# Sink attention and a multiplicative FFN on one core: the sink values by eight small transfers and a head mask, and a new order of pieces, loads and tasks

## The chip, the cores and the metric

The kernel runs on one core of one Trainium2 chip. The metric is the device time of one execution in microseconds. Three timed runs of the kernel before are given, and one profiled execution, from which all views below are taken.

## The reference

Four batches of eight heads, 768 positions, 64 numbers to a head. Each query sees the first four keys (the sinks) and the 128 keys up to itself. The result of all heads, 3072 rows of 512, goes through a multiplicative feed-forward layer whose last two matrices are not separated by a nonlinearity.

```python
scores = scale * np.matmul(q, k.transpose(0, 1, 3, 2))
keep = (pos[None, :] < n_sink) | ((rel >= 0) & (rel < window))   # n_sink = 4, window = 128
a = softmax(np.where(keep, scores, -1e9))
x = np.matmul(a, v)                    # then rows of 512: all heads of one position
h = (x @ w1) * (x @ w2) @ w3           # 512 -> 1024 -> 1024
out = h @ w_out                        # 1024 -> 512, all in float32
```

## The kernel before, in words

**Stages.** The kernel multiplies w3 and w_out once into one matrix, `w3o` (1024 x 512). For that each of the eight row blocks of w3 is transposed on the PE (`fold_w3`, L408), copied to SBUF by the DVE as `w3t` (L413; two of them lie in free room of the tiles `kN` and `qN` of batch 1), and multiplied with the rows of w_out (`fold_mm`, L438, into PSUM tiles `ph` and `pw`). Then, for each batch: the keys and queries are transposed (batches 0 and 1 on the PE, L211, with a copy L213; batches 2 and 3 by transposing DMAs, L218), the scores are computed (`sc`, L261 and L282), the ScalarE (ACT) takes the exponential (L266, L286), the DVE applies the window mask (L270, L290), the values are multiplied in (`av`, L314 and L351), the DVE divides by the sum, and the result is transposed to `xT` (by the PE for batch 0 and a transposing DMA, L378, for the others). Two "gates" a block, `pg` (L391), give x@w1 and x@w2; ACT copies the one and the DVE multiplies it with the other (L395, L398). At last `project` multiplies with `w3o` (`po`, L452), and the output goes out by a DMA from SyncE (SP, L459).

**Sinks.** Scores against the four sink keys of all heads come from `sink_scores` (L243). The sink values of batch b lie in `vs`, one row of 128 for each of the sinks of each head: head pair r and its half e have rows 32r+4e to 32r+4e+3, zero elsewhere, with a column for the sum. They are made in `sink_values`: one PE matmul `vp` (L232) with a 0/1 matrix `pick` spreads the first four rows of `vN` to all groups of rows, and the DVE multiplies with the head mask `ones_s` (L234).

**Loads.** SP first issues nine transfers of 512 KB, the `raws`: four pieces of w_out (two row blocks each) and five row blocks of w3, in float32, to tiles that are not used yet (`homes`: `ab`, `kN`, `qN`, `kqT`). ACT or DVE casts each to bfloat16 (L418). All other loads are issued by GpSimd (POOL) with a cast on the way, in the order of the list `order`: the blocks of 128 positions of q, k and v, the other three blocks of w3, w1 and w2. POOL begins once the fifth of the raws has landed (`hold`, L201).

**The order of the work.** Each step is a `task` with its engine times, its predecessors and a priority. `plan` goes through the tasks and lets each engine take the one that can start first by the planner's own cost numbers; `landings` says when the planner thinks that loads arrive, and `keep_busy` (L466) puts matmuls on zeros, `pz`, into gaps at the start. `PACE` holds score tasks apart. What `plan` gives is written out as a fixed order of instructions for PE, ACT, DVE and SP, and each engine works through its own list in that order. So an engine that waits with one instruction holds up all that stand behind it.

Of the kernel before, what the change touches and what calls it, by code (L numbers as in the profile page):

```python
# [21 lines left out]
def kernel(  # L22
# [13 lines left out]
    nc = tc.nc  # L36
# [16 lines left out]
    CHUNKS = [[(256 * i, 256 * i + 256) for i in range(3)]] * 2 + [[(0, 384), (384, 768)]] * (B - 2)  # L53
    XPOSE = (2, 3)
    BLOCKS = ((0, 0), (0, 1))
# [71 lines left out]
    def load(what, *i):  # L127
# [21 lines left out]

    nudge = {}  # L150

# [21 lines left out]
    nc.vector.memset(maskt[:], 1.0)  # L173
    nc.vector.memset(pick[:], 0.0)
    for b in range(B - 1):
# [53 lines left out]
    def sink_values(b):  # L229

        vp = ps_mm.tile([P, H, D], FP32, tag="mm", name="vp")
        nc.tensor.matmul(vp[:], pick[:], vN[b][:, 0, :, 0:D], start=True, stop=True)  # L232
        yield
        nc.vector.tensor_mul(vs[b][:, :, 0:D], vp[:],  # L234
                             ones_s[:].rearrange("p (h o) -> p h o", o=1).to_broadcast([P, H, D]))
        yield
# [187 lines left out]
    def folded(i):  # L424
        return ("fm", i, len(FM[i]) - 1)
# [42 lines left out]

    arrive = {}

    def service(what, *i):
# [8 lines left out]

    def landings(taken, RAW=2.0, POOL=3.0, DGE=1.3, RAMP=(0.6, 0.95, 0.85, 0.9)):

        queues = {"sp": [(RAW, 1.28, 1.0, [("raw",) + x[:3]]) for x in raws],
                  "pool": [(gen, us, 1.8, keys) for x in order for gen, us, keys in service(*x)]}
# [4 lines left out]
        while any(at[n] < len(q) for n, q in queues.items()):  # L489
# [17 lines left out]
            for n in busy:  # L507
                i = int(now - RAW) if now >= RAW else 0
                share = 1.0 if len(busy) == 1 else 0.5 if small not in "kqv" else 0.79 if n == "sp" else 0.13
                left[n][at[n]] -= 0.02 * share * (RAMP[i] if i < len(RAMP) else 1.0)  # L510
                if left[n][at[n]] <= 0.0:
                    lag, keys = queues[n][at[n]][2:]
                    for key in keys:
                        arrive[key] = now + lag
                    if n == "pool":
                        landed.append(now + lag)
                    at[n] += 1
# [11 lines left out]
    made = {}  # L529
    for n, ((what, i0, i1, e), ap) in enumerate(zip(raws, casts)):  # L530
        task(("c", what, i0), n, cast(e == "act", *ap), [(e, 1.04 if e == "act" else 0.69)],
             loads=[("raw", what, i0, i1)])
        made.update({(what, i): ("c", what, i0) for i in range(i0, i1)})

    def need(what, i):
        return ([made[what, i]], []) if (what, i) in made else ([], [(what, i)])

    for i in range(KFF):
        for h in range(2):
            j0, j1 = 4 * h, 4 * h + 4  # L540
            needs = [need("w3", i)]
# [20 lines left out]
    for b in range(B):  # L562
        for t in range(NT):
# [3 lines left out]
            for kb in kbs:  # L567
                if b in XPOSE:
                    for n, src, dst in (("k", kN[b], kT[b]), ("q", qN[b], qT[b])):
# [7 lines left out]
            if t == 0:  # L577
                task(("sk", b), 0, sink_keys(b), [("dve", 0.2)], [("sc", b, 1, 0)])
                task(("sv", b), 2, sink_values(b), [("pe", 0.22), ("dve", 0.7)],
                     [("av", b - 2, NP - 1, NT - 1), ("av", b, 1, 0)] if b >= 2 else [], [("v", b, 0)], "mm")  # L580
            else:
# [3 lines left out]
                elif t == 1:  # L585
                    more = [(n, b, kb) for n in (("tdk", "tdq") if b in XPOSE else ("tpk",)) for kb in (4, 5)]
                    task(("ss", b, 1), -1, sink_scores(b, 1, NT), [("pe", 0.225), ("act", 0.6)],
                         qk + more + [("sk", b)], ring="mm", started=[("sc", b, 1, 1)])
# [21 lines left out]
            for r in range(NP):  # L610
                after = list(qk)
                if b >= 2 and t == 0:
                    after.append(("g", b - 2, len(CHUNKS[b - 2]) - 1, KFF - 1, 1))
                lead = r % 2 == 0
# [20 lines left out]
    for b in range(B):  # L635
        for c, (t0, t1) in enumerate(CHUNKS[b]):
            last_t = (t1 - 1) // 256
            us = 0.65 * (t1 - t0) / 384
            for dt in range(KFF):
                n = dt * P // 256  # L640
                pr = 1000 + 200 * b + 10 * c + dt
                war = [("p", b - 2, NB - 1)] if b >= 2 else []
                task(("g", b, c, dt, 0), pr + 0.5, gate(b, c, dt, 0), [("pe", us), ("act", 0.2 + us / 2)],
                     ([("xd", b, last_t, 0), ("xd", b, last_t, 1)] if (b, last_t) in X_XPOSE else
                      [("xt", b, NP - 2, last_t)]) + war, [("w1", n), ("w2", n)], "mm",
                     [("g",) + gates[-2] + (1,)] if len(gates) > 1 else [])
# [3 lines left out]
            for m in range(t0 // P, t1 // P):  # L650
                cuts = (0, DM // 2, 3 * DM // 4, DM) if (b, m) == (B - 1, NB - 1) else (0, DM)
                for n0, n1 in zip(cuts, cuts[1:]):
# [3 lines left out]
                          ("act", 0.1) if n0 > DM // 2 else ("sp", SP_US)],  # L656
                         [("g", b, c, KFF - 1, 1), *[folded(i) for i in range(KFF)]], ring="mm")

# [10 lines left out]
    def plan(emit):  # L669
# [16 lines left out]
        def pe_pick():  # L686
            best = None
            for k in tasks.values():
# [16 lines left out]
                if k["paced"]:  # L705
                    busy = max(0.0, free["act"] - free["pe"]) + sum(q[2] for q in queue["act"])
                    est = max(est, free["pe"] + busy - BACKLOG, last_sc + (PACE[k["name"][1]]))
                wait = est - free["pe"]
# [124 lines left out]
```

## Time and profile before

| | us |
|---|---|
| timed runs: median (lowest, highest) | 198.28 (197.68, 198.59) |
| profiled execution: time | 197.16 |
| profiled execution: span from first to last instruction | 195.5 |
| PE busy | 187.9 (96%) |
| DVE, ACT, POOL busy | 115.2, 104.2, 75.5 |
| granted TensorE clock | 1.0 throughout |

The profiled execution takes 1.7 us more than its span, and it is 1.1 us below the median of the timed runs. A row of the timeline gives start, length, engine, line, operation and what it reads and writes; a length of several matmuls is that of the group, and the last of a group overlaps the next, so that what PE spends is read from one start to the next. In brackets stands how long the engine was idle before, and who released it. PEld is the loading of weights, which runs ahead of PE. The chain of waits lists pieces that led to the end, in order of time.

### The profile page before, as it was taken

Reading aid. Unit: us, or ns where it says so; the run is one execution under the profiler, and the core shown is the slowest. Engines: PE = TensorE matmul, PEld = TensorE weight load, DVE = VectorE, ACT = ScalarE, POOL = GpSimd, SP = SyncE. Lnnn points to the kernel's source line nnn. Section 1 sums busy time; section 2 is a strip of 40 time slices with the busy share of each in tenths; the row PEclk is TensorE's granted clock in tenths of the full one; section 3 lists DMA queues with packets and bytes.
Section 4 is the critical chain, followed back from the end, with each engine's and each line's share of the span. In section 5 each row is a group of like instructions: output and inputs, shape, how many; then the busy total and the mean of one; then the engine's idle time right before and its main releaser. Section 6 shows DMA issues by size and latency. Waiting matters only on the chain.

```text
span 195.5 us, 4615 instructions
## 1 busy us (share of the span) xinstructions
PE 187.9 (96%) x1818; PEld 123.4 (63%) x1831; DVE 115.2 (59%) x276; ACT 104.2 (53%) x176; POOL 75.5 (39%) x104
## 2 busy tenths in 40 slices
PE   7689999999999999999999999999999999999993
PEld 2245566888776687888886555566666666644443
DVE  4456696755989888678575426678788344410000
ACT  4242569635776876565565646657583333333232
POOL 5189967689999953433553330000000000000000
PEclk9999999999999999999999999999999999999999
DMA  6999999999999999999999999999220200014334
GB/s 225 401 362 156 179 162 197 194 159 154 155 150 183 180 176 114 156 159 145 137 155 155 149 159 191 239 208 155 49 54 2 57 0 0 0 57 161 143 134 152
DMA packets 107429, 29.14 MB, mean 149 GB/s; under 512 B 98448, under 2 KB 102928, under 8 KB 107408
## 3 DMA queue, kind: packets, MB, share of 16 engines
q0 software_dynamic: 79520, 12.33, 90.3%
q1 hardware_dynamic: 27744, 16.46, 40.6%
q8 instruction: 14, 0.23, 0.5%
q10 hardware_dynamic: 144, 0.07, 0.1%
q14 instruction: 7, 0.06, 0.1%
HBM read 29.36 MB, written 6.29 MB: 182 GB/s over the span
## 4 chain that ended last, share of the span: by engine, by line
PE 86%; DMA 7%; POOL 3%; DVE 1%; issue 1%; SPq 1%; ACT 0%; DVEq 0%
PE pg L391 39%; PE po L452 21%; PE av L351 6%; PE sc L261 5%; DMA ab<-in_moe_w_dram 4%; PE pw L438 4%; DMA qN<-in_q_dram 3%; PE ph L438 3%; PE tp L211 2%; PE tp L408 2%; PE av L314 1%; PE sc L282 1%; POOL vN L108 1%; POOL qN L108 1%; POOL kN L108 1%; PE sp L243 1%
## 5 line engine op out<-in xcount | busy, mean ns | idle before, releaser
L391 PE MATMUL pg<-xT,w_sb 128*128 128x256 bf16 (+1 forms) x640 | 91.5, 294 | 0.0
L391 PEld LDWEIGHTS <-w_sb 128*128 128x128 bf16 x640 | 59.7, 98 | 20.2 <-issue 0.9
L398 ACT COPY a_sb<-pg 128x256 f32<-128x256 f32 (+1 forms) x80 | 33.2, 415 | 40.2 <-PE pg L391 22.7
L395 DVE TENSOR_TENSOR ab<-a_sb,pg 128x256 bf16<-128x256 f32 (+1 forms) x80 | 37.8, 472 | 25.5 <-PE pg L391 21.2
L452 PE MATMUL po<-w3o,ab 128*128 128x512 bf16 (+2 forms) x200 | 42.7, 362 | 0.4
L266 ACT ACTIVATE ex<-sc 128x1024 bf16<-128x1024 f32 (+1 forms) x40 | 38.0, 962 | 5.7 <-PE sc L261 3.9
L452 PEld LDWEIGHTS <-ab 128*128 128x128 bf16 x208 | 19.1, 98 | 20.6 <-issue 0.6
L270 DVE TENSOR_TENSOR am<-ex,maskt 128x1024 bf16<-128x1024 bf16 (+1 forms) x40 | 25.4, 646 | 5.3 <-ACT ex L266 5.2
L108 POOL DMA_DIRECT2D kN<-in_k_dram x24 | 22.4, 931 | 12.8 <-DMA qN<-in_q_dram 10.1
L456 ACT COPY w_sb<-po 128x512 f32<-128x512 f32 (+2 forms) x25 | 14.1, 564 | 24.2 <-PE po L452 24.2
L108 POOL DMA_DIRECT2D qN<-in_q_dram x24 | 22.1, 921 | 9.9 <-DMA vN<-in_v_dram 7.4
L108 POOL DMA_DIRECT2D vN<-in_v_dram x24 | 21.9, 912 | 7.2 <-DMA kN<-in_k_dram 5.1
L358 DVE TENSOR_TENSOR xn<-av,rec 128x256 bf16<-128x256 f32 x40 | 17.0, 425 | 1.4
L351 PE MATMUL av<-vN,am 128*128 128x65 bf16 x296 | 16.7, 193 | 0.0
L351 PEld LDWEIGHTS <-am 128*128 128x128 bf16 x296 | 14.4, 97 | 2.1 <-DVE am L270 0.2
L355 DVE RECIPROCAL rec<-av 128x4 f32<-128x4 f32 x40 | 7.2, 179 | 10.3 <-PE av L351 9.9
L456 DVE COPY w_sb<-po 128x128 f32<-128x128 f32 x1 | 0.3, 292 | 19.7 <-ACT w_sb L456 19.7
L261 PE MATMUL sc<-kqT 64*128 64x128 bf16 (+1 forms) x216 | 11.6, 238 | 0.0
L351 PE MATMUL av<-vs,es 128*128 128x130 bf16 x56 | 11.1, 220 | 0.0
L213 DVE COPY kqT<-tp 128x1024 bf16<-128x1024 bf16 x12 | 8.3, 689 | 3.2 <-PE tp L211 3.1
L438 PE MATMUL ph<-wo_sb,w3t 128*128 128x512 bf16 x31 | 8.0, 380 | 2.0 <-ACT wo_sb L418 1.3
L286 ACT ACTIVATE ex<-sc 128x1024 bf16<-128x1024 f32 x7 | 7.0, 1026 | 5.3 <-PE sc L282 5.3
(71 smaller groups left out, 136.0 us busy)
## 6 DMA issues: line engine op xcount, KB each, us to landing
out_dram<-w_sb SPq DMA_DIRECT2D x23, 256.0 KB, 5.0
kN<-in_k_dram POOLq DMA_DIRECT2D x24, 128.0 KB, 8.0
qN<-in_q_dram POOLq DMA_DIRECT2D x24, 128.0 KB, 8.1
vN<-in_v_dram POOLq DMA_DIRECT2D x24, 128.0 KB, 7.9
w_sb<-in_moe_w_dram POOLq DMA_DIRECT2D x9, 256.0 KB, 8.6
ab<-in_moe_w_out_dram SPq DMA_DIRECT2D x3, 512.0 KB, 6.2
ab<-in_moe_w_dram SPq DMA_DIRECT2D x3, 512.0 KB, 7.0
kN<-in_moe_w_out_dram SPq DMA_DIRECT2D x1, 512.0 KB, 9.3
```

Of the source, the lines that this page charges most:

```text
L108: nc.gpsimd.dma_start(out=dst, in_=rows(src, b, kb))
L261: nc.tensor.matmul(sc[:, e, c:c + n], kT[b][hp, r, kb * P:(kb + 1) * P], qT[b][hp, r, qb * P:qb * P + n], start=True, stop=True)
L266: nc.scalar.activation(ex[:, :, c0:], sc[:, :, c0:], ACTF.Exp, scale=scale)
L270: nc.vector.tensor_mul(am[:, :, c0:], ex[:, :, c0:], mk)
L351: nc.tensor.matmul(o, lhs, rhs, start=(n == 0), stop=(n == len(todo) - 1), skip_group_check=True)
L358: nc.vector.tensor_mul(xns[b, t][:, :, r, :, :], av[:, :, :, 0:D], rec[:].to_broadcast([P, 2, 2, D]))
L391: nc.tensor.matmul(pg[:], w_sb[:, kk, dt * P:(dt + 1) * P], xT[b][:, kk, tk], start=(kk == 0), stop=(kk == NP - 1))
L395: nc.vector.tensor_mul(ab[b][:, dt, tk], gate_a.pop((b, c, dt))[:], pg[:])
L398: nc.scalar.copy(a_sb[:], pg[:])
L438: nc.tensor.matmul(po, w3T[i][:, j, :], wo_sb[:, j, :], start=(j == 0), stop=(j == KFF - 1))
L452: nc.tensor.matmul(po[:], ab[b][:, kk, m * P:(m + 1) * P], w3o[:, kk, n0:n1], start=(kk == 0), stop=(kk == KFF - 1))
L456: (nc.vector.tensor_copy if n0 == DM // 2 else nc.scalar.copy)(o_sb, po[:])
```

## The change

Five things change, and line numbers shift by up to four.

1. `pick`, its two POOL copies and the four matmuls `vp` go. In their place SP issues eight small transfers, right behind the raws, each of which brings the four sink rows of one head for all batches (4 partitions x 4 batches x 64 floats) to a float32 tile `vc`, cleared by a memset before. `sink_values` is the DVE multiplication alone, with `vc` for all heads and the mask `ones_s`.
2. The nine raws come in another order, and some are cast by another engine; two are cast in halves, one half on DVE and one on ACT ("both").
3. POOL loads block 5 of w3 ahead of the first block of q, k and v instead of behind it.
4. The planner's numbers change: landing model, cast costs, `PACE` by batch and by third of the batch, four priorities (`nudge`), predecessors named one by one instead of the last of a group.
5. As a consequence the fixed order is another on every engine. `XPOSE` is written in another way and holds the same pairs.

```diff
-    pick = const.tile([P, P], BF16, name="pick")
+    vc = const.tile([P, B, D], FP32, name="vc")
...
-    raws = [("wo", 0, 2, "act"), ("w3", 0, 1, "dve"), ("wo", 2, 4, "act"), ("w3", 1, 2, "dve"),
-            ("wo", 4, 6, "act"), ("w3", 2, 3, "dve"), ("wo", 6, 8, "act"), ("w3", 3, 4, "dve"), ("w3", 4, 5, "dve")]
+    raws = [("wo", 2, 4, "act"), ("w3", 4, 5, "act"), ("w3", 0, 1, "both"), ("wo", 0, 2, "dve"),
+            ("w3", 1, 2, "dve"), ("wo", 4, 6, "dve"), ("wo", 6, 8, "dve"), ("w3", 2, 3, "both"),
+            ("w3", 3, 4, "act")]
...
-    order = [("qkv", 0, 0, 1), ("w3", 5, 6), ("qkv", 0, 1, 2), ("w3", 6, 8), ("qkv", 0, 2, 3),
+    order = [("w3", 5, 6), ("qkv", 0, 0, 1), ("qkv", 0, 1, 2), ("w3", 6, 8), ("qkv", 0, 2, 3),
...
-    nudge = {}
+    nudge = {("g", 0, 2, 6, 0): -300, ("g", 1, 2, 4, 0): -1200, ("g", 0, 1, 3, 1): 60, ("fm", 6, 3): 1500}
...
-    pk = pick[:].rearrange("p (r x) -> p r x", x=32)
-    for e in range(2):
-        nc.gpsimd.tensor_copy(pk[:, :, 4 * e:4 * e + 4],
-                              ident[:, 0:4].rearrange("p (r s) -> p r s", r=1).to_broadcast([P, NP, 4]))
+    for h in range(H):
+        r0 = 32 * (h // 2) + 4 * (h % 2)
+        nc.sync.dma_start(out=vc[r0:r0 + 4, :, :], in_=v[:, h, 0:4, :].rearrange("b s d -> s b d"))
...
     def sink_values(b):
 
-        vp = ps_mm.tile([P, H, D], FP32, tag="mm", name="vp")
-        nc.tensor.matmul(vp[:], pick[:], vN[b][:, 0, :, 0:D], start=True, stop=True)
-        yield
-        nc.vector.tensor_mul(vs[b][:, :, 0:D], vp[:],
+        nc.vector.tensor_mul(vs[b][:, :, 0:D], vc[:, b:b + 1, :].to_broadcast([P, H, D]),
                              ones_s[:].rearrange("p (h o) -> p h o", o=1).to_broadcast([P, H, D]))
...
+        cuts = ((0, 1024, e),) if e in ("act", "dve") else ((0, 512, "dve"), (512, 1024, "act"))
+        for c0, c1, eng in cuts:
...
-                task(("sv", b), 2, sink_values(b), [("pe", 0.22), ("dve", 0.7)],
-                     [("av", b - 2, NP - 1, NT - 1), ("av", b, 1, 0)] if b >= 2 else [], [("v", b, 0)], "mm")
+                task(("sv", b), 2, sink_values(b), [("dve", 0.6)],
+                     [("av", b - 1, 1, NT - 1)] if b else [], [("vc",)])
...
-    PACE = [0.0, 2.6, 5.5, 4.5]
+    PACE = [[0, 1.3, 0], [0, 0, 0], [6.2, 0, 0], [5.3, 0, 0]]
```

Three places of the order show what moves. The first is the start, on DVE. L418 (L415 after) casts a raw, L413 (L410 after) copies a transposed piece of w3; `ab`, `qN`, `kqT` and `kN` are the homes of raws here, `w_sb` is w3 and `wo_sb` w_out. Before:

```order
L418 CAST w_sb<-ab_103 128x1024
L413 COPY w3t<-tp_197 128x512
L413 COPY w3t<-tp_202 128x512
L418 CAST w_sb<-ab_104 128x1024
L413 COPY w3t<-tp_218 128x512
L413 COPY w3t<-tp_223 128x512
L418 CAST w_sb<-ab_104 128x1024
```

After:

```order
L410 COPY kN_88<-tp_203 128x512
L410 COPY kN_88<-tp_208 128x512
L415 CAST w_sb<-ab_103 128x512
L415 CAST wo_sb<-ab_104 128x1024
L410 COPY w3t<-tp_220 128x512
L410 COPY w3t<-tp_225 128x512
L415 CAST w_sb<-ab_104 128x1024
L415 CAST wo_sb<-ab_104 128x1024
```

The first cast of w3 has gone to ACT, and DVE has casts of w_out in its row, of which one stands ahead of the two copies of the second transposed piece.

The second place is the sink values. On PE, in batch 1, before (`vN_1_92` is the v tile of that batch, and the gates around it are those of batch 0):

```order
L391 LDWEIGHTS w1_sb_78
L391 MATMUL pg_914<-xT_0_99,w1_sb_78 128x256
L232 LDWEIGHTS pick_74
L232 MATMUL vp_921<-vN_1_92,pick_74 128x512
L391 LDWEIGHTS w2_sb_79
L391 MATMUL pg_926<-xT_0_99,w2_sb_79 128x256
```

On DVE, in batch 0, after (`kqT_95` are that batch's transposed keys and queries):

```order
L410 COPY qN_84<-tp_299 128x512
L410 COPY qN_84<-tp_308 128x512
L213 COPY kqT_95<-tp 128x8x128
L231 TENSOR_TENSOR vs_111<-vc,ones_s 128x8x64
L410 COPY w3t<-tp_329 128x512
L410 COPY w3t<-tp_349 128x512
```

PE no longer waits for a v tile to make the sink values; DVE waits for the eight small transfers, with copies behind it that PE needs.

The third place is SP's row in the middle of the kernel, where outputs of batch 0, transposes of batch 1's results (`xT_100`) and transposes of batch 2's keys (`kN_89`) and queries (`qN_85`) stand in one row. From the third block's key transpose on, before:

```order
L218 DMA_TRANSPOSE kqT_97<-kN_89 128x4x128
L378 DMA_TRANSPOSE xT_100<-xn 128x4x128 x2
L218 DMA_TRANSPOSE kqT_97<-qN_85 128x4x128
L459 DMA out_dram<-w_sb 128x512
L378 DMA_TRANSPOSE xT_100<-xn 128x4x128 x2
L218 DMA_TRANSPOSE kqT_97<-kN_89 128x4x128
L218 DMA_TRANSPOSE kqT_97<-qN_85 128x4x128
```

After:

```order
L218 DMA_TRANSPOSE kqT_97<-kN_89 128x4x128
L375 DMA_TRANSPOSE xT_100<-xn 128x4x128 x2
L456 DMA out_dram<-w_sb 128x512
L218 DMA_TRANSPOSE kqT_97<-qN_85 128x4x128
L456 DMA out_dram<-w_sb 128x512
L218 DMA_TRANSPOSE kqT_97<-kN_89 128x4x128
L375 DMA_TRANSPOSE xT_100<-xn 128x4x128 x2
L218 DMA_TRANSPOSE kqT_97<-qN_85 128x4x128
```

One output more stands ahead of the fourth block's query transpose, which is the last row of both.

More of the change, by code (lines that the diff above doesn't have):

```diff
@@ L469 @@
     arrive = {}
+    arrive["vc",] = 20.0
     def service(what, *i):
@@ L479, in service, with landings @@
         return [(0.8, 1.34 * (i[1] - i[0]), [(w,) + (n,) for n in range(i[0], i[1])]) for w in ("w1", "w2")]
-    def landings(taken, RAW=2.0, POOL=3.0, DGE=1.3, RAMP=(0.6, 0.95, 0.85, 0.9)):
-        queues = {"sp": [(RAW, 1.28, 1.0, [("raw",) + x[:3]]) for x in raws],
+    def landings(taken, RAW=2.0, POOL=3.0, DGE=1.3, RAMP=(0.75, 1.0)):
+        queues = {"sp": [(RAW, 1.28, 1.0 if n < 2 else 1.9, [("raw",) + x[:3]]) for n, x in enumerate(raws)],
                   "pool": [(gen, us, 1.8, keys) for x in order for gen, us, keys in service(*x)]}
@@ L513, in landings @@
                     for key in keys:
-                        arrive[key] = now + lag
+                        arrive[key] = now + lag + min(2.5, max(0.0, 0.25 * (now - 36.0)))
                     if n == "pool":
@@ L529, with need @@
     made = {}
[L530 to L536, printed above, removed]
+    for n, ((what, i0, i1, e), (dst, src)) in enumerate(zip(raws, casts)):
+        cuts = ((0, 1024, e),) if e in ("act", "dve") else ((0, 512, "dve"), (512, 1024, "act"))
+        for c0, c1, eng in cuts:
+            name = ("c", what, i0, c0)
+            us = (c1 - c0) / 1024
+            task(name, n, cast(eng == "act", dst[:, c0:c1], src[:, c0:c1]),
+                 [(eng, 0.16 + 0.88 * us if eng == "act" else 0.07 + 0.62 * us)], loads=[("raw", what, i0, i1)])
+            for x in range(c0 // 512, c1 // 512):
+                made[(what, i0, x) if what == "w3" else (what, i0 + x, 0)] = name
+    def need(what, i, h=0):
+        return ([made[what, i, h]], []) if (what, i, h) in made else ([], [(what, i)])
     for i in range(KFF):
@@ L540 @@
             j0, j1 = 4 * h, 4 * h + 4
-            needs = [need("w3", i)]
+            needs = [need("w3", i, h)]
             task(("t3", i, h), 100 + i + (5 if i < SPLIT and h else 0), fold_w3(i, j0, j1),
@@ L585 @@
                 elif t == 1:
-                    more = [(n, b, kb) for n in (("tdk", "tdq") if b in XPOSE else ("tpk",)) for kb in (4, 5)]
+                    more = [(n, b, kb) for n in (("tdk", "tdq") if (b, 2) in XPOSE else ("tpk",)) for kb in (4, 5)]
                     task(("ss", b, 1), -1, sink_scores(b, 1, NT), [("pe", 0.225), ("act", 0.6)],
@@ L612 @@
                 if b >= 2 and t == 0:
-                    after.append(("g", b - 2, len(CHUNKS[b - 2]) - 1, KFF - 1, 1))
+                    after += [("g", b - 2, len(CHUNKS[b - 2]) - 1, dt, 1) for dt in range(KFF)]
                 lead = r % 2 == 0
```

17 lines of the change are left out of this document (9 added, 8 removed).

## The prediction

> **What bounds the kernel now.** I read the page first, then the stretches, then the timeline of each engine over the first 60 us, and last the chain of waits. In the page the first line is the span, the second the engines' busy time. In the stretches the columns are length, PE, PEld, DVE, ACT and POOL busy (with counts), granted clock, DMA share and GB/s.
>
> ```profile
> span 195.5 us, 4615 instructions
> PE 187.9 (96%) x1818; PEld 123.4 (63%) x1831; DVE 115.2 (59%) x276; ACT 104.2 (53%) x176; POOL 75.5 (39%) x104
> ...
> 25.10:60.00 34.90, 34.52 (x442) 27.04 (x447) 26.34 (x64) 22.78 (x41) 29.45 (x37) 1.00 2.17 167
> 60.00:150.00 90.00, 89.73 (x982) 62.59 (x984) 64.30 (x162) 56.63 (x99) 29.05 (x34) 1.00 1.54 148
> 150.00:192.50 42.50, 42.32 (x249) 23.22 (x247) 10.32 (x20) 14.89 (x30) 0.00 (x0) 1.00 0.21 71
> ```
>
> From 25.1 us on PE is busy for 166.57 of 167.4 us at the full granted clock. So PE bounds the kernel, and behind 25 us there are two things to gain: fewer matmuls, and about a microsecond of waits. Before 25 us PE waits for pieces of w3 and w_out. These rows are of ACT, DVE, POOL and PE (start, length):
>
> ```profile
> 4.18 1.04 ACT L418 CAST wo_sb<-ab 128x1024 bf16<-128x1024 f32 x1 [2.10 <-DMA ab<-in_moe_w_out_dram]
> 5.42 0.71 DVE L418 CAST w_sb<-ab 128x1024 bf16<-128x1024 f32 x1 [1.82 <-DMA ab<-in_moe_w_dram]
> 7.93 1.04 ACT L418 CAST wo_sb<-ab 128x1024 bf16<-128x1024 f32 x1 [2.70 <-DMA ab<-in_moe_w_out_dram]
> 9.21 0.69 DVE L418 CAST w_sb<-ab 128x1024 bf16<-128x1024 f32 x1 [1.83 <-DMA ab<-in_moe_w_dram]
> 11.75 0.69 DVE L418 CAST w_sb<-ab 128x1024 bf16<-128x1024 f32 x1 [0.60 <-DMA ab<-in_moe_w_dram]
> 15.96 1.04 DVE L418 CAST w_sb<-kqT 128x1024 bf16<-128x1024 f32 x1
> ...
> 25.36 0.75 POOL L111 DMA_DIRECT2D w_sb<-in_moe_w_dram  x1 [1.16 <-DMA w_sb<-in_moe_w_dram]
> ...
> 24.81 0.53 PE L330 MATMUL xt<-ident,xn 128*128 128x128 bf16 x4
> 25.17 0.70 PE L408 MATMUL tp<-ident,w_sb 128*128 128x128 bf16 x8
> ```
>
> The raws are cast as they land: the first at 4.18, the second at 5.42, the third at 7.93, the fourth at 9.21, the sixth at 11.75, the ninth by 15.96. A late fixed point is the last load of w3 (blocks 6 and 7, by POOL): POOL is released by a w3 load at 25.36, and PE begins to transpose that piece at 25.17, with hardly a wait.
>
> **The start.** The new order of raws brings the same number of bytes in the same queue, so I take the landings by place in the queue. First piece to transpose: cast by ACT from 5.42 for 1.04, so 6.46, where DVE was done at 6.13. That is 0.33 later. The next piece lands third, at 7.93; halves on two engines take some 0.4 to 0.6 (an estimate from the 0.69 and 1.04 of whole casts). The first product needs the first row blocks of w_out, which land fourth: 9.21 plus 0.69 on DVE is 9.9. From there to the first transposes of blocks 6 and 7 the order has 48 products, 48 transposes, two score groups and eight value matmuls on PE. By starts in these rows, where a group ends when the next begins:
>
> ```profile
> 22.77 0.43 PE pw L438 x2
> 22.32 0.45 PE tp L211 x8
> 20.37 0.33 PE sc L282 x8
> 24.09 0.23 PE av L314 x4
> 88.70 0.22 PE vp L232
> ```
>
> a product takes 0.215, a transpose 0.056, a group of eight scores 0.33 and 0.09 more on the way in (below). That is 10.3 + 2.7 + 0.8 + 0.25 = 14.1, so PE is there at 24.0; with two waits of some 0.25 (for the DVE cast of the sixth raw, 11.75 + 0.69, and for the block of w3 that POOL now loads first) at 24.5. The load is there at 25.1 as before, since the same bytes are moved ahead of it. So the start, with its late first product, costs nothing and brings nothing: 0.6 us of slack covers it, and if the slack is gone each further microsecond counts in full. The 0.33 and the casts that moved are hidden in it. The next loads tie both kernels in the same way, so I set the start to equal at 25.1.
>
> **PE's work behind that point.** I count what stands in PE's row behind the first transposes of blocks 6 and 7. Before it holds 20 products `pw`, 3 `vp`, 168 score matmuls of 128 columns and 20 transposes `xt`; after 16, none, 176 and 24. All else is equal, 26 visits to the scores against 24 apart. What a visit costs beside its matmuls is read from these rows:
>
> ```profile
> 28.82 0.55 PE sc L282 x16
> ...
> 53.87 0.60 PE L391 MATMUL pg<-xT,w_sb 128*128 128x256 bf16 x4
> 54.31 0.22 PE L351 MATMUL av<-vs,es 128*128 128x130 bf16 x1
> ...
> 54.67 0.60 PE L391 MATMUL pg<-xT,w_sb 128*128 128x256 bf16 x4
> 55.20 0.50 PE L261 MATMUL sc<-kqT 64*128 64x256 bf16 x8
> ...
> 35.23 0.22 PE xt L330 x4
> ```
>
> Eight scores take 0.33 and sixteen 0.55, so 0.11 is not theirs; and four gates take 0.44 ahead of values, but 0.53 ahead of scores. A visit costs 0.20. The sum: four products less, -0.86; three `vp` less, -0.66; eight scores more, +0.22; two visits more, +0.40; four `xt` more, +0.22. Together -0.68. The first of the four `vp` stood ahead of 25.1 and brings nothing.
>
> **Waits that go.**
>
> ```profile
> 48.61 0.60 PE L391 MATMUL pg<-xT,w_sb 128*128 128x256 bf16 x4
> 49.30 0.39 PE L232 MATMUL vp<-vN,pick 128*128 128x512 bf16 x1
> 53.17 0.39 PE L211 MATMUL tp<-ident,kN 128*128 128x128 bf16 x4
> 53.64 0.40 PE L211 MATMUL tp<-ident,qN 128*128 128x128 bf16 x4
> ...
> 49.30 0.10 PEld L232 LDWEIGHTS <-pick 128*128 128x128 bf16 x1 [0.37 <-DMA vN<-in_v_dram]
> 53.64 0.23 PEld L211 LDWEIGHTS <-qN 128*128 128x128 bf16 x4 [0.25 <-DMA qN<-in_q_dram]
> ```
>
> The four gates from 48.61 end at 49.05, and `vp` starts at 49.30, released by batch 1's first v load: 0.25 of wait, which goes with `vp`. The query transposes of batch 1's third block wait 0.25 for their load as well. Before, 120 gate matmuls stand ahead of them; after, 128 and a whole output block of eight `po`, which is 2.6 us more; less four `pw` and the `vp`, PE comes about 1.5 us later to them. So this wait goes too, with some margin. Sum so far: -0.68 - 0.25 - 0.25 = -1.18.
>
> **Waits that come.** Batch 2's second third of scores needs the fourth block's query transpose by DMA:
>
> ```profile
> 81.17 0.53 SPq L459 DMA_DIRECT2D out_dram<-w_sb  x1
> 86.96 1.71 SPq L218 DMA_TRANSPOSE kqT<-qN  x1
> ...
> DMA to landing us min/median/max: 7.8/7.9/8.0
> ...
> 95.83 0.55 PE sc L261 x12
> ```
>
> The middle line is the answer for `kqT` transposes issued from 86 to 88 us. Issue at 86.96 plus 7.9 is 94.9, and the scores start at 95.83, so there is 0.9 of slack. After, PE has the same work up to there (within 0.1) and none of the two waits, so it comes at 95.3. SP has one output more ahead, 0.53 and 0.09 to the next: 95.5. That is a wait of 0.2, between 0 (if SP's row runs earlier, since its key transposes move up) and 2 (if an output and two result transposes that came before now delay it by their own 0.5 and 1.3 to 1.7 each). I take 0.2, the row's own shift. The sum for the profiled execution is -1.0.
>
> **The small transfers.** On SP eight issues of 0.44 each (the row of the ninth raw below) end near 9.4, and SP has nothing else until 58 us. Their data stand behind the ninth raw in the queue. DVE comes to `vs` behind the copy of the first transposed block, at some 19.6 as before:
>
> ```profile
> 5.20 0.44 SPq L162 DMA_DIRECT2D kqT<-in_moe_w_dram  x1
> ...
> 19.62 0.69 DVE L234 TENSOR_TENSOR vs<-vp,ones_s 128x512 bf16<-128x512 f32 x1
> ...
> out_dram<-w_sb SPq DMA_DIRECT2D x1, 64.0 KB, 1.7
> ```
>
> If they land like the smallest transfer of the trace, 1.7 us behind the ninth raw (cast at 15.96), that is 17.7, hidden by 1.9 us. The multiplication itself stays at 0.69 off the bound. The Trainium skill ("DMA: Bandwidth & Descriptors", anatomy of one DMA) puts about 2.0 us of fixed cost on each DMA, and its specifications ask for at least 512 B a piece, where these have 256 B. No row of this trace shows an SP load in such small pieces. By the 2.0 us, counted once, they would land at 18.0, which changes nothing; counted eight times, one after another, they would come still later than in the second rival below.
>
> **From the profiled execution to the median.** The profiled execution is 1.12 us under the median. No view says where the timed runs lose this. If loads land later in them, the kernel before has no slack at 48 to 54 us, and the changed one has 1.5. I put a third of the 1.12 there, -0.4, between 0 and -1.1. Forecast: 198.28 - 1.0 - 0.4 = 196.9.
>
> **Rivals.** A measurement of this kernel can tell about 0.5% (1.0 us) from no change.
>
> First, the gain is given back on SP's queue and by other reordered waits: the query transpose of block four lands not at 95.5 but at 96.3 or more, and 1 us of the gain is gone; 197.3 to 198.9. For it speaks that SP is in use nearly without a break from 63 to 105 us and that its transposes need 8 us; against it, that PE's order holds the same amount of work ahead of these scores.
>
> Second, slower: the small transfers go one after another. Eight times 1.7 behind 15.96 is 29.6. DVE stands at `vs` from 19.6, and behind it stand copies of w3 and the copy of the second transposed block, without which PE has no more scores and no products. It decides from a landing at 20.2, which is the 0.6 of slack; at 29.6 it costs 9.4, so 206 us; at 22.5, as if half of them overlapped badly, 2.3 less the gain of 1.0, so 199.6. Against it: the raws, from the same queue, were issued long ahead of their landing and landed 1.28 apart from 7.93 to 9.21, so transfers of a queue overlap their latency.
>
> Third, more: all of the 1.12 was lateness of loads and goes: 196.2; if w3's last load also comes earlier, by up to the 0.6 us of slack that the start has, 195.6.
>
> **How the numbers follow.** Forecast, 196.4 to 197.3: 0.38. First rival: 0.35. Second, with half of it mild: 0.13. Third: 0.14. So faster by over 0.5% is 0.38 + 0.14 = 0.52, within 0.35, slower 0.13. The range reaches from 195.5 to 199.0; it leaves out most of the second rival and a little of the third.
>
> **What would show it.** Right: no wait of PE above 0.2 at the third block of batch 1; no `vp`; the transposes of w3's last blocks at 25.1; the scores of batch 2's second third at 95.3 to 95.5; PE's end 1.0 us earlier. Wrong: DVE idle ahead of `vs` and PE idle behind it near 20 us; PE late to 25.1; a PE wait for `kqT` near 95 us above 1 us.

## The result, and the profile after

The changed kernel takes 196.73 us (median; 194.90 to 199.46), the kernel before 198.26 us (196.97 to 199.20) on the same chip. The ratio is 0.9905, with a 95% interval of 0.9883 to 0.9928: faster by 0.95%, or 1.5 us by the medians. The forecast was 196.9 us. A ratio is taken from undisturbed executions alone, those within 1.5% of the fastest of their kernel, so where a kernel's times fall into two groups it can differ from the ratio of the medians.

The profiled execution of the changed kernel takes 196.08 us, with a span of 194.4 us, which is 1.1 us less than before. The page's first rows, and below them the same three stretches as before; the last one ends 3.0 us ahead of the end of the span, as it did there (columns: length, PE, PEld, DVE, ACT and POOL busy with counts, granted clock, DMA share, GB/s).

```profile
span 194.4 us, 4625 instructions
PE 188.2 (97%) x1830; PEld 123.7 (64%) x1830; DVE 114.4 (59%) x277; ACT 103.9 (53%) x177; POOL 75.6 (39%) x102
...
25.10:60.00 34.90, 34.90 (x447) 27.29 (x444) 26.74 (x65) 22.74 (x41) 29.80 (x37) 1.00 2.10 170
60.00:150.00 90.00, 89.83 (x999) 62.92 (x996) 64.67 (x166) 56.82 (x98) 28.56 (x34) 1.00 1.53 146
150.00:191.40 41.40, 41.33 (x239) 22.54 (x237) 9.60 (x18) 14.52 (x29) 0.00 (x0) 1.00 0.21 73
```

PE is busy for 166.06 of 166.30 us behind 25.1 us; before it was 166.57 of 167.40. The stretch is 1.10 us shorter, but these busy times do not split it into work and waits. The page of before has 1818 matmuls beside 1831 weight loads, the page of after 1830 beside 1830: thirteen matmul records are missing from the trace of before. Eight are products `po`, as the groups show, before and then after (count, busy, mean ns, idle ahead of them):

```profile
L452 PE MATMUL po<-w3o,ab 128*128 128x512 bf16 x176 | 41.0, 379 | 0.4
L449 PE MATMUL po<-w3o,ab 128*128 128x512 bf16 x184 | 41.2, 379 | 0.0
```

Where such a record is missing, the trace shows some 0.05 us of idle time that was none (0.4 for the eight `po`). Eleven of the thirteen stand behind 25.1 us, so about 0.6 of the 0.83 us of idle time of before are not waits. By starts, two waits that the prediction names have gone, 0.25 and 0.24 us, and one of about 0.34 us has come; the other 0.95 us of the 1.10 are PE's work and small pauses. These rows of PE (start, length, last in brackets the wait) answer to the places that the prediction names:

```profile
25.18 0.39 PE L405 MATMUL tp<-ident,w_sb 128*128 128x128 bf16 x4
...
55.01 0.39 PE L211 MATMUL tp<-ident,kN 128*128 128x128 bf16 x4
55.23 0.39 PE L211 MATMUL tp<-ident,qN 128*128 128x128 bf16 x4
...
94.94 0.23 PE L258 MATMUL sc<-kqT 64*128 64x128 bf16 x2
95.34 0.56 PE L258 MATMUL sc<-kqT 64*128 64x256 bf16 x10 [0.17 <-DMA kqT<-qN]
```

The last blocks of w3 are transposed from 25.18 us, as before (25.17). The third block of batch 1 has no wait: keys at 55.01, queries right behind at 55.23. The scores of batch 2's second third wait for their query transpose: behind the first pair at 94.94 there is a hole of about 0.3 us, of which 0.17 stand in brackets, and the rest follow at 95.34.

The small transfers, by the rows of the tile `vc` (duration of an issue in ns: min/median/max; first and last start), and DVE at the multiplication that reads it:

```profile
L199 SPq DMA_DIRECT2D vc<-in_v_dram x8: 250/250/313, 6.0 to 14.9; - x8
...
19.25 0.68 DVE L231 TENSOR_TENSOR vs<-vc,ones_s 128x512 bf16<-128x512 f32 x1
```

DVE starts at 19.25 with no wait in brackets, so the transfers are hidden. But their issues do not end near 9.4: eight issues spread from 6.0 to 14.9 are 1.27 us apart, the step at which the raws land.

One wait is new and was not forecast. These rows are of PE and, the last, of its weight loads, which run ahead of it:

```profile
20.62 0.39 PE L211 MATMUL tp<-ident,kN 128*128 128x128 bf16 x4
22.11 0.40 PE L211 MATMUL tp<-ident,qN 128*128 128x128 bf16 x4 [1.10 <-DMA qN<-in_q_dram]
...
25.00 0.39 PEld L405 LDWEIGHTS <-w_sb 128*128 128x128 bf16 x4 [0.15 <-DMA w_sb<-in_moe_w_dram]
```

PE comes to the query transposes of batch 0's second block at 20.84 (20.62 and four transposes of 0.056) and waits for their load. It costs next to nothing in this execution: the last load of w3 lands only at about 25.0, where the weight load waits for it, and PE reaches 25.18 in time.

### The profile page after: what moved, and what is told of

It reads as the page before. It is cut to its first block, busy times and chain, and to the rows that moved or that the text cites. A ratio compares the mean times of both kernels' runs of the same rounds, so it can differ in the third digit from the quotient of the medians.

```text
span 194.4 us, 4625 instructions
## 1 busy us (share of the span) xinstructions
PE 188.2 (97%) x1830; PEld 123.7 (64%) x1830; DVE 114.4 (59%) x277; ACT 103.9 (53%) x177; POOL 75.6 (39%) x102
## 4 chain that ended last, share of the span: by engine, by line
PE 82%; DMA 11%; POOL 3%; SPq 2%; issue 0%; DVE 0%; ACT 0%; DVEq 0%
PE pg L388 39%; PE po L449 21%; PE av L348 6%; PE sc L258 5%; DMA kqT<-qN 4%; DMA ab<-in_moe_w_dram 4%; DMA qN<-in_q_dram 3%; PE tp L211 3%; PE pw L435 2%; PE av L311 1%; PE sc L279 1%; SPq L375 1%; PE ph L435 1%; SPq L163 1%; PE sp L240 1%; POOL qN L108 1%
## 5 line engine op out<-in xcount | busy, mean ns | idle before, releaser
L108 POOL DMA_DIRECT2D qN<-in_q_dram x24 | 22.1, 919 | 9.9 <-DMA vN<-in_v_dram 6.2
L258 PEld LDWEIGHTS <-kqT 64*128 64x128 bf16 x216 | 7.0, 94 | 4.6 <-issue 4.0
```

What stands on the lines that cost most here:

```text
L108: nc.gpsimd.dma_start(out=dst, in_=rows(src, b, kb))
L258: nc.tensor.matmul(sc[:, e, c:c + n], kT[b][hp, r, kb * P:(kb + 1) * P], qT[b][hp, r, qb * P:qb * P + n], start=True, stop=True)
```

## The experiments

Three theories stand in the expectations. A: the landings of loads are fixed points, so the end is set by the last load that PE waits for and by PE's work behind it. B: PE's work alone counts. C, formed once the first results were in: the change is worth what it is only in the order that came with it; each new plan of the kernel makes its own waits, between 75 and 140 us, for transposing DMAs.

### Each part alone, planned anew

The changed kernel again, beside the first three experiments:

> The changed kernel once more, beside its experiments. Both theories: 0.9905 of the kernel before, 196.3 to 197.1 us. If the spread of its runs comes from loads that land differently from one execution to the next, this profile shows other waits of PE for loads before 30 us than the first (there 1.27 us for the second block's queries), and PE's end differs by about their difference.

196.37 us (195.05 to 198.13), ratio 0.9919 (0.9881 to 0.9956). The gain is repeated. This profiled execution has a span of 195.2 us, 0.8 more than the first, so one profile tells a gain of this size only roughly. The early loads do not make the difference: the wait for the second block's queries is 0.65 us here, not 1.10, and PE is at the last blocks of w3 at 25.04. It is a wait for a transposing DMA in batch 3, which the first profile does not have:

```profile
138.80 0.56 PE L258 MATMUL sc<-kqT 64*128 64x256 bf16 x10 [0.78 <-DMA kqT<-qN]
```

**Sinks alone**: the kernel before with the small transfers, without `pick` and `vp`; the planner makes its own order.

```diff
-        vp = ps_mm.tile([P, H, D], FP32, tag="mm", name="vp")
-        nc.tensor.matmul(vp[:], pick[:], vN[b][:, 0, :, 0:D], start=True, stop=True)
-        yield
-        nc.vector.tensor_mul(vs[b][:, :, 0:D], vp[:],
+        nc.vector.tensor_mul(vs[b][:, :, 0:D], vc[:, b:b + 1, :].to_broadcast([P, H, D]),
...
-                task(("sv", b), 2, sink_values(b), [("pe", 0.22), ("dve", 0.7)],
-                     [("av", b - 2, NP - 1, NT - 1), ("av", b, 1, 0)] if b >= 2 else [], [("v", b, 0)], "mm")
+                task(("sv", b), 2, sink_values(b), [("dve", 0.6)],
+                     [("av", b - 1, 1, NT - 1)] if b else [], [("vc",)])
```

> The kernel before with the small transfers in place of pick and vp, all else (order of raws and loads, casts, PACE) as before; the planner plans anew. Theory A, the clock of the loads: PE ends at the latest of a load's landing plus PE's work behind it. By the landings of the profile before, the query load of batch 1's third block (53.59) still binds, and behind it stands 0.52 us less work than before: -0.5 us, 197.8. PE waits more for batch 1's blocks than before (0.25), about 0.8 in sum. Theory B, PE's work: three vp behind 25 us, one visit less and the wait at vp go, -0.66 - 0.2 - 0.25: -1.1 us, 197.1, and nothing waits more.

206.39 us (205.06 to 208.84), ratio 1.0427 (1.0356 to 1.0497): 8 us slower, and both theories are far off. PE's waits from 15 to 150 us (total, times, longest), then PE and the chain of waits around the longer of them:

```profile
PE pg L387 <- DMA xT<-xn: 6.8, 2, 4.5
PE tp L210 <- DMA qN<-in_q_dram: 0.4, 1, 0.4
```

```profile
119.62 1.90 PE L448 MATMUL po<-w3o,ab 128*128 128x512 bf16 x7
126.04 1.44 PE L387 MATMUL pg<-xT,w_sb 128*128 128x384 bf16 x4 [4.51 <-DMA xT<-xn]
...
117.08 8.71 DMA xT<-xn
```

The gates of batch 2 need the transposed result `xT`; its transposing DMA is issued at 117.08 and lands 8.71 us later. These gates are next in PE's row, and PE stands for 4.51 us. The other 2.28 us of the 6.8 stand at 89.01, ahead of gates of batch 1.

**The order alone**: the changed kernel with `pick` and `vp` put back and the transfers taken out (the diff above, reversed), planned anew.

> The changed kernel with pick and vp put back in place of the small transfers, all else as changed; the planner plans anew. Theory A: the latest of landing plus work is 0.7 us earlier than before and 1.1 later than in the changed kernel: 197.6. Theory B: four vp more, 0.86 over the changed kernel: 197.6. The two do not differ in the sum here; A says that PE waits for batch 0's blocks and B that it never waits for a load behind 25 us.

The twelve executions take 198.34 to 203.79 us, with a median of 202.41; three of them are below 199 us, at a granted clock of 1.00, and the other nine show 0.983 to 0.992. The ratio of 1.0054 (1.0002 to 1.0107) is that of the four lowest alone. The profiled execution is the lowest, at 198.34, and has one wait of PE that stands out; the slower ones have no trace:

```profile
PE pg L392 <- DMA xT<-xn: 1.9, 1, 1.9
```

**The old loads**: the changed kernel with the lists `raws` and `order` of before, planned anew.

> The changed kernel with the old lists of raws (order and casting engine) and of POOL's loads, all else as changed; the planner plans anew. Theory A: behind the queries of batch 0's fifth block (landing 42.98) stand 2.1 us more of PE's work than in the changed kernel: 2.1 us slower, 198.8, slower than the kernel before. Theory B: PE's work behind 25 us is 0.36 more than in the changed kernel: 197.1.

202.21 us (200.53 to 202.93), ratio 1.0207 (1.0154 to 1.0259). A had the direction, but neither the size nor the place:

```profile
PE pg L387 <- DMA xT<-xn: 1.9, 1, 1.9
PE sc L257 <- DMA kqT<-qN: 1.7, 2, 1.3
PE tp L210 <- DMA qN<-in_q_dram: 0.5, 1, 0.5
```

What follows: in the three profiles most of the added time is in waits for transposing DMAs (`xT<-xn`, `kqT<-qN`), not in the parts under test. So these runs compare plans, not parts, and A and B, which leave out the middle of the kernel, do not decide here.

Why a plan goes wrong there can be read in the planner. It prices a transposing DMA by `8.4 if at < end - 4.0 else 5.0 if at < end else 2.7`, where `end` is its own reckoning of the last load. With its numbers written out, the pair of the wait above is finished on SP at 113.35 and 114.65 in the plan of the sinks alone, with `end` at 116.76: past 112.76, so it is priced at 5.0 behind its issue of 1.3, 6.3 in all, where the trace has 8.71. In the plan of the kernel before it is finished at 111.46 and 112.76, with `end` at 119.16, and priced at 8.4. The pair of the order alone is priced at 5.0 as well. But the pairs behind the waits at 89.01 in the sinks alone and at 89.77 (1.94 us) in the old loads were priced at 8.4, so the step can account for a part of the waits at most. That it is a cause was not tried by a run.

### The sink values in a fixed order

**In the order of before**: the task keeps its time on PE in the plan, and only the matmul is not issued. PE's row is that of before less four `vp`.

```diff
-        vp = ps_mm.tile([P, H, D], FP32, tag="mm", name="vp")
-        nc.tensor.matmul(vp[:], pick[:], vN[b][:, 0, :, 0:D], start=True, stop=True)
         yield
-        nc.vector.tensor_mul(vs[b][:, :, 0:D], vp[:],
+        nc.vector.tensor_mul(vs[b][:, :, 0:D], vc[:, b:b + 1, :].to_broadcast([P, H, D]),
```

> The kernel before with the eight small transfers and without pick and vp, and with its order kept: the task of the sink values keeps its place and its PE time in the plan, only the matmul is not issued, so every engine's row is that of the kernel before less four vp. Theory C (each part alone was slow because the planner made another order, not because of the part): no new wait between 75 and 140 us, clock 1.0, and a small gain. Its size by the work of PE alone: 4 x 0.22, 197.4. By the loads as the fixed points (the query load of batch 1's third block at 53.6 binds, two vp stand behind it): 197.9. Rival (the small transfers themselves disturb SP's queue or the DVE): again above 203, with waits for xT between 85 and 140 us.

198.02 us (196.89 to 199.69), beside 198.13 of the kernel before; ratio 1.0004 (0.9970 to 1.0037). The 8 us are gone, so they belonged to the plan and not to the transfers. But 0.9 us of PE's work has left the row and the time is the same. Rows of PE and of one weight load of this kernel:

```profile
25.38 0.62 PE L405 MATMUL tp<-ident,w_sb 128*128 128x128 bf16 x8 [0.57 <-DMA w_sb<-in_moe_w_dram]
...
51.03 0.40 PE L210 MATMUL tp<-ident,qN 128*128 128x128 bf16 x4 [0.33 <-DMA qN<-in_q_dram]
...
53.62 0.40 PE L210 MATMUL tp<-ident,qN 128*128 128x128 bf16 x4
53.62 0.23 PEld L210 LDWEIGHTS <-qN 128*128 128x128 bf16 x4 [0.26 <-DMA qN<-in_q_dram]
...
123.62 0.82 PE L388 MATMUL pg<-xT,w_sb 128*128 128x384 bf16 x4 [0.96 <-DMA xT<-xn]
```

Before, the last query transposes of batch 1's third block stood at 53.64; now they stand at 53.62. Two `vp` and one wait for v had gone ahead of them, and waits for w3's last load and for two q loads took it all back. That is what theory A says, read from one execution. The other two `vp`, 0.44 us, were lost at 123.62, to an `xT` that came late in this execution (its span is 196.4 us, 0.9 above that of before). These two rows of SP (the first of before, the second of this kernel) show where:

```profile
113.45 2.68 SPq L378 DMA_TRANSPOSE xT<-xn  x2
```

```profile
112.20 1.19 SPq L217 DMA_TRANSPOSE kqT<-qN  x1
...
115.04 2.80 SPq L375 DMA_TRANSPOSE xT<-xn  x2
```

The `xT` pair is issued 1.6 us later than before, behind key and query transposes in SP's row.

**In the order of after**: `vp` put back into the changed kernel's order, each just ahead of the multiplication that reads it.

```diff
+        vp = ps_mm.tile([P, H, D], FP32, tag="mm", name="vp")
+        nc.tensor.matmul(vp[:], pick[:], vN[b][:, 0, :, 0:D], start=True, stop=True)
-        nc.vector.tensor_mul(vs[b][:, :, 0:D], vc[:, b:b + 1, :].to_broadcast([P, H, D]),
+        nc.vector.tensor_mul(vs[b][:, :, 0:D], vp[:],
```

> The changed kernel with its order kept and pick and the four vp matmuls put back in it, each issued just ahead of the multiplication that reads it; the eight small transfers are gone. Theory C: slower than the changed kernel by PE's work, 0.66 to 0.88, so 197.1 to 197.6, with clock 1.0 and no wait above 0.5 behind 100 us. Rival (the order alone does not pay without the small transfers, because vp waits for v tiles): 198.3 to 203, as with the part planned anew.

197.36 us (196.88 to 199.26), ratio 0.9985 (0.9954 to 1.0016), against 0.9905 (0.9883 to 0.9928) with the transfers. So here taking out the four `vp` is worth 0.6 to 1.0 us by the medians (taken on different chips) and 1.6 us by the ratios, and this order with `vp` in it is worth nothing that can be measured. Neither part brings a gain by itself; together they bring 0.95%.

But what `vp` costs here is not PE's work alone. Rows of DVE and PE of this kernel, and then the same multiplication on DVE in the changed kernel:

```profile
58.54 0.69 DVE L234 TENSOR_TENSOR vs<-vp,ones_s 128x512 bf16<-128x512 f32 x1 [1.30 <-PE vp L233]
59.15 1.15 DVE L270 TENSOR_TENSOR am<-ex,maskt 128x1024 bf16<-128x1024 bf16 x2
59.88 0.30 PE L351 MATMUL av<-vN,am 128*128 128x65 bf16 x4 [0.66 <-DVE am L270]
```

```profile
57.47 0.68 DVE L231 TENSOR_TENSOR vs<-vc,ones_s 128x512 bf16<-128x512 f32 x1
```

Batch 1's `vp` stands late in PE's row, DVE waits 1.30 us for it, the window mask behind it comes late, and PE waits 0.66 us for the mask. In this profile that wait weighs as much as the three `vp` behind 25 us (0.65). This order was planned without `vp`; what it would bring with that `vp` further ahead was not tried.

### The loads earlier

One number changes; PE's order stays as it is. POOL waits for the fourth (or third) raw instead of the fifth.

```diff
-        nc.gpsimd.tensor_copy(spent[:], casts[hold - 1][1][:, 0:1])
+        nc.gpsimd.tensor_copy(spent[:], casts[hold - 2][1][:, 0:1])
```

In the changed kernel:

> The changed kernel, same order on PE; POOL begins its loads when the fourth raw has landed instead of the fifth, so about 1.28 us earlier. Theory A (landings hold the start and the first 55 us, PE's work counts only behind the last load that PE waits for): the query load at 22.1 us and w3's last load at 25.0 land up to 1.0 us earlier, the wait of 1.26 us at 22.1 shrinks, and the time falls by 0.3 to 1.0, to 195.6 to 196.4. Rival (the raws are slowed by the earlier loads as much as those gain, since the bytes are the same): within 0.3 of the changed kernel, 196.4 to 197.0, with the first transposes and products later instead.

196.15 us (195.57 to 197.11), ratio 0.9890 (0.9856 to 0.9925). POOL is released at 8.95 instead of 9.79 us, 0.84 earlier and not 1.28. The wait at 22.1 us is gone, and one for the queries of batch 0's first block has come:

```profile
19.12 0.40 PE L211 MATMUL tp<-ident,qN 128*128 128x128 bf16 x4 [0.33 <-DMA qN<-in_q_dram]
...
25.16 0.39 PE L405 MATMUL tp<-ident,w_sb 128*128 128x128 bf16 x4
```

PE is at the last blocks of w3 at 25.16, where it was at 25.18: what the loads gained was lost ahead of them, as the expectation's rival has it. The time falls into A's range, but by the interval it cannot be told from the changed kernel, 0.9905.

> As the one before, with POOL's loads from the third raw on, about 2.5 us earlier than in the changed kernel. Theory A: no better than the one before by more than 0.3, since the raws now share the transfer engines for longer and w_out's and w3's first pieces come later: 195.4 to 197.0. Rival: 197 to 198.5, slower than the changed kernel by the lateness of the raws.

With `hold - 3`, 196.19 us (195.84 to 197.06), ratio 0.9889 (0.9857 to 0.9922): no further gain. No wait for q is left, and its place is taken by waits for DVE, for casts of w3 and copies of its transposed pieces:

```profile
PE tp L405 <- DVE w_sb L415: 0.5, 1, 0.5
PE ph L435 <- DVE w3t L410: 0.5, 1, 0.5
```

In the kernel before, and in the kernel before without `vp` in its own order:

> The kernel before, same order; POOL begins its loads one raw earlier (about 1.28 us). Theory A: its binding loads (v at 49.3 and q at 53.6 us, 0.25 us each, and w3's last at 25.2) come earlier and the waits go: 0.3 to 0.6 faster, 197.5 to 197.8. Rival (PE's work alone, or loads no earlier): within 0.2 of the kernel before.

> The kernel before without vp, in its own order (as the run e1b_sinks_same_order, which gained nothing), with POOL's loads one raw earlier. Theory A: with the loads earlier the four vp now count, so it is faster than the kernel before with loads earlier alone by 0.4 to 0.9, and than the kernel before by 0.7 to 1.4: 196.7 to 197.4. Rival (the vp were worth nothing for another reason, as the results' transposes that come 1.1 us late at 123.6 us): equal to the kernel before with the loads earlier, 197.5 to 198.1, with a wait for xT near 123 us.

With `vp` 197.96 us (196.33 to 198.48), ratio 0.9971 (0.9941 to 1.0001); without `vp` 197.42 us (196.34 to 198.72), ratio 0.9952 (0.9921 to 0.9982). The step that gained nothing gains some 0.5 us by the medians once the loads come earlier. That is what A says, but the two intervals overlap, and the last one's profiled execution still has waits of 0.7 us for `kqT` and 0.5 us for `xT`.

### Two rivals priced

**SP's row**: two outputs of batch 0 are issued by ACT instead of SP, ahead of batch 2's transposes.

```diff
-        (nc.scalar if n0 > DM // 2 else nc.sync).dma_start(out=out[t0:t0 + P, n0:n1], in_=o_sb)
+        (nc.scalar if n0 > DM // 2 or (b, m) in ((0, 3), (0, 4)) else nc.sync).dma_start(out=out[t0:t0 + P, n0:n1], in_=o_sb)
```

> The changed kernel with two of batch 0's outputs (rows m = 3 and 4) issued by ACT instead of SP; PE's row is the same. They stand in SP's row ahead of the key and query transposes of batch 2. Theory C (SP's row delays those transposes): the transposes are issued some 0.6 to 1.2 us earlier, the wait of 0.34 us at the scores at 95.3 us goes, and the time falls by 0.2 to 0.4, to 196.0 to 196.5 where the changed kernel has 196.4 to 196.7. Rival (the transposes' 8 us from issue to landing, which other transfers make, set it): no change within 0.2, with the wait still there or moved; slower by up to 0.5 if ACT's issues delay its exponentials.

196.78 us (195.27 to 197.97), ratio 0.9924 (0.9886 to 0.9962): no gain. SP's rows, of this kernel and then of the changed one:

```profile
83.49 5.05 SPq L375 DMA_TRANSPOSE xT<-xn  x2
88.63 1.27 SPq L218 DMA_TRANSPOSE kqT<-qN  x1
```

```profile
83.44 4.05 SPq L375 DMA_TRANSPOSE xT<-xn  x2
87.58 1.57 SPq L218 DMA_TRANSPOSE kqT<-qN  x1
```

The query transpose is issued no earlier, but 1.05 us later: the `xT` pair ahead of it takes longer than the outputs saved. The time is as the expectation's rival has it, no change; what holds the pair was not tried.

**More small transfers**: 32, one for each batch and head, instead of eight.

```diff
-        nc.sync.dma_start(out=vc[r0:r0 + 4, :, :], in_=v[:, h, 0:4, :].rearrange("b s d -> s b d"))
+        for b in range(B):
+            nc.sync.dma_start(out=vc[r0:r0 + 4, b, :], in_=v[b, h, 0:4, :])
```

> The changed kernel with 32 small transfers (one for each batch and head, 4 pieces of 256 B each) instead of eight; order the same. It measures the price of the prediction's second rival. If the issues run one behind another and each waits for the transfer eight places earlier, the last lands at 23 to 27 us, DVE waits 4 to 8 us at vs, and PE, whose waits for loads before 25 us hide some 1 to 2 us of it, comes 2 to 6 us later: 199 to 203. If they overlap as the raws do (0.44 us an issue, from 14.9 on), the last lands near 27 as well, with the same price. If the wait is absorbed by the loads that PE waits for anyway: 196.5 to 197.5.

208.70 us (206.99 to 212.02), ratio 1.0520 (1.0464 to 1.0576). SP, DVE and PE:

```profile
5.63 23.37 SPq L200 DMA_DIRECT2D vc<-in_v_dram  x32
```

```profile
31.02 0.69 DVE L232 TENSOR_TENSOR vs<-vc,ones_s 128x512 bf16<-128x512 f32 x1 [11.25 <-DMA vc<-in_v_dram]
```

```profile
21.54 0.40 PE L212 MATMUL tp<-ident,qN 128*128 128x128 bf16 x4
32.10 1.04 PE L436 MATMUL ph<-wo_sb,w3t 128*128 128x512 bf16 x2 [10.16 <-DVE w3t L411]
```

This is the prediction's second rival, at its place and with its chain: DVE stands at `vs`, the copies of w3 stand behind it, PE stands for 10.16 us, and the kernel is 12 us slower than the changed one. The added 24 issues take SP to 29.00 us; from 15.15, where eight issues end (14.9 and 0.25), that is 0.58 us each. The absorption that one branch of the expectation allowed is not there, and its other branches, 199 to 203, were too low: they put the landing at 23 to 27 us, where DVE starts at 31.02, and left out that the clock falls to half behind such a wait (last section), which costs some 3 us more by an estimate.

## Why the prediction was right, point by point

- **The start equal at 25.1**: right, 25.18 against 25.17. The path there was another: the first raw of w3 was cast at 5.92 and the third raw at 7.20, not at 5.42 and 7.93, and PE waited 1.10 us at 22.11 instead of the two waits of 0.25 that the prediction had placed. The slack of 0.6 us was used up by that wait, and just sufficed.
- **PE's work, -0.68**: right in its counts. Behind the first transposes of w3's last blocks the changed kernel has 16 products, no `vp`, 176 score matmuls of 128 columns and 24 `xt`, as counted. By starts, work and small pauses together are 0.95 us less; the 0.27 beyond the forecast are not assigned. The busy times (-0.51) mislead here, for the records that the trace of before lacks.
- **About a microsecond of waits to gain**: too much. The 0.83 us of idle time that the prediction read holds about 0.6 us of missing records; by starts, 0.5 us of waits were there. The sum did not use the microsecond.
- **Two waits that go, -0.25 each**: right, in both profiles of the changed kernel. Batch 1's third block was forecast at some 1.5 us later than 53.64, and stands at 55.23, without a wait.
- **The wait that comes, +0.2 at 95.3**: right in place and nearly in size, 0.17 in brackets and about 0.3 by the starts. The issue is 0.62 us later than before (87.58 against 86.96), the shift that the prediction took. That the one more output in SP's row is the reason is not confirmed: with two outputs taken out of the row, the issue came no earlier.
- **The sum for the profiled execution, -1.0**: measured -1.08, by 197.16 less 196.08. In the second profiled execution it is -0.3. The sum was not better than the spread between executions of the same kernel, so that it agrees to 0.1 us is in part luck.
- **From the profile to the median, -0.4**: the distance between the two was 1.12 us and is 0.65 now (196.73 less 196.08), so the term has the right size, by luck: in the second run of the changed kernel the profiled execution lies 0.53 us above the median (196.90 and 196.37). That late loads in the timed runs are the reason was only argued, and no run shows it.
- **The small transfers hidden**: right by 2 us, with a wrong timing of SP. The landing was forecast for 17.7; the end of the last issue at 15.15 and the 2.0 us from there to DVE's start in the kernel with 32 transfers give an estimate of 17.2. The Trainium skill ("DMA: Bandwidth & Descriptors", anatomy of one DMA) has about 2.0 us for the fixed part of one DMA, in a section on transfers that GpSimd issues; these come from SP. The trace with 32 transfers is near it, with 2.02 us (29.00 to 31.02), counted once and not once for each transfer.
- **The first rival**, SP's queue and reordered waits: in the changed kernel it came in one of two profiles, with 0.78 us at 138.80 and not at 95, and the median held all the same; it came in every kernel that was planned anew, with 1.9 to 6.8 us. The prediction's price, 1 us or a little more, was too low for these. The order that came with the change has less of such waits, which the prediction did not say.

## What to carry to other kernels

In a kernel whose order is written out by a planner, a part taken alone is not the part but another plan: hold the order fixed and leave out or put back the one instruction. Work that is removed from the bounding engine pays only where no load or transfer stands as a fixed point behind it; here it paid nothing in the old order and 0.6 to 1.0 us in the new one, a wait of DVE included, and the new order paid nothing without it. When one instruction is put back, look where it lands: late in its row, it brings waits of its own. Compare the counts of matmuls and weight loads before idle time is read from busy time: a missing record looks like a wait. Before adding a transfer to a queue that gates an engine early on, count its issues: eight were free, 32 cost 12 us.

## What the runs showed of the hardware

**The clock falls behind a gap of PE.** Stretches of the sinks alone (PE stood from 121.5 to 126.04), and of the kernel with 32 transfers (from 21.9 to 32.10); the granted clock is the third column from the right:

```profile
122.00:125.00 3.00, 0.00 (x0) 0.00 (x0) 0.34 (x1) 0.15 (x1) 0.00 (x0) 1.00 1.65 144
125.00:127.00 2.00, 0.96 (x4) 0.49 (x5) 0.00 (x0) 0.00 (x0) 0.00 (x0) 0.72 1.43 227
127.00:129.00 2.00, 2.00 (x16) 1.31 (x15) 0.61 (x2) 0.48 (x1) 0.00 (x0) 0.50 1.46 219
129.00:131.00 2.00, 2.00 (x26) 1.14 (x25) 1.07 (x3) 0.53 (x2) 0.00 (x0) 0.92 1.41 235
```

```profile
20.00:25.00 5.00, 1.84 (x23) 1.09 (x22) 0.00 (x0) 1.02 (x1) 4.31 (x6) 0.93 1.74 178
...
31.00:34.00 3.00, 1.90 (x5) 0.74 (x6) 2.55 (x5) 0.00 (x0) 2.04 (x3) 0.50 1.45 196
34.00:37.00 3.00, 2.79 (x20) 1.22 (x20) 0.35 (x2) 1.61 (x2) 1.75 (x2) 0.50 1.45 196
37.00:40.00 3.00, 2.99 (x36) 2.17 (x36) 2.42 (x7) 2.32 (x3) 2.06 (x3) 0.83 1.80 180
```

By the means of the stretches, if the clock is either full or half, it falls to half some 4.4 us behind the last matmul in the one and 2.4 us in the other, and stays there for some 3.3 and 6 us after PE has begun again. So a wait costs more than its length: half of these times, some 1.6 and 3 us, is an estimate of what was lost besides. The gap of 1.9 us in the order alone left the clock at 1.00 in its profile. The Trainium skill ("TensorE: Matmul & The Clock Gate", HAM oscillation) asks for no gap of PE above about 3.4 us. The runs agree in part, with full clock behind 1.9 us and half behind 4.5; the 2.4 us of the other kernel are less than the skill's 3.4, and no run here shows why.

**A row of issues takes longer than its issues.** Eight issues of 0.25 us each took 9 us behind nine raws, 1.27 us apart, and 24 more took 0.58 us each. That the queue's earlier transfers hold them fits the 1.27 us, about the step at which raws land (1.28, as the prediction has it), but was not tried. An issue's own length says little about when a row of them is done.
